# A third batch cut to 64 of 96 token rows, one-hot masks moved between two stages, and low weight halves made by accumulating DMAs

## The chip, the cores and the metric

The kernel runs on one core of a Trainium2 chip. The metric is device time in microseconds (us). A core has five engines that run side by side and meet at semaphores: TensorE (PE in the profile, PEld for its weight loads), VectorE (DVE), ScalarE (ACT), GpSimd (POOL) and SyncE (SP, which here only issues DMAs). Each engine works through its own instructions in their order; DMAs are issued from the queues of SP, ACT and POOL.

## The reference

```python
Y = np.fft.rfft(x, axis=1) * (filt_r + 1j * filt_i)[None]      # x: 8 batches x 3072 tokens x 256
x = np.fft.irfft(Y, n=3072, axis=1).reshape(8 * 3072, 256)     # the tokens of the second half
logits = x @ w_gate                                            # 8 experts
expert_idx = np.argmax(logits, axis=1)
gate_w = softmax(logits)[expert_idx]                           # per token
for i in range(N):                                             # in token order
    e = expert_idx[i]
    if counts[e] < capacity:                                   # 768 per expert
        disp[e, counts[e]] = x[i]; counts[e] += 1; keep[i] = True
y = relu(disp[e] @ w1[e]) @ w2[e]                              # 256 -> 1024 -> 256
out[i] = gate_w[i] * y[expert_idx[i], pos[i]] if keep[i] else 0
```

A convolution over each batch by Fourier transform, then a mixture of experts in which every expert takes its first 768 tokens and all other rows of the output are zero. So the kernel needs only as many tokens, from the start, as fill all eight experts. It transforms three of the eight batches, counts, and has a slow branch (`tc.If(least < cap)`) that does the other batches if some expert is not full by then.

## The kernel before, in words

**The transform.** A batch is 3072 tokens, laid out as 96 rows (`N1`) of 32 (`N2`). Token n is row n // 32, column n % 32. Six steps on TensorE, methods of `Conv`: `a` (matrix over the 96 rows), `t` (transposes), `b` (matrix over the 32 columns, then the complex product with the filter on DVE and POOL, lines 267 to 272), `g` (transpose back together with the gate matrix, so that 16 logit columns come along), `bi` (inverse over 32) and, outside the class, `ai` (inverse over 96, line 353), whose result is tokens in 96 rows. `ai` works in two halves of the 272 columns, `HS`: half 0 has 144 columns (128 channels and the 16 logit sums), half 1 has 128. ACT copies each bank of PSUM to an `rt` buffer (line 355, five buffers), SP stores it to `ybuf` in HBM (line 359), and for half 0 an addition makes the logits `L` (line 358). An fp32 matrix is recorded as two passes. Transposes of `V` (`ti`, line 342) on DVE stand between `bi` and `ai`. `middle` strings `b`, `g` and `bi` together and runs short lists of other work in ten places between, handed over as `fill`.

**Routing.** `route` returns steps: `counts` (maximum, one-hot and running sum of a batch on DVE), `sums` (two small matrices on TensorE that carry counts over rows and batches, line 410), `slots` (each token's place), four `masks` (one-hot matrices in fp16 for 8 of the 32 columns each, lines 455 to 457) and `table` (8 matrices for each mask, line 465, which scatter token numbers into the table `tacc` of slots).

**Experts.** A chunk is 384 slots of one expert; an expert has two, (e,0) and (e,1). `gather` fetches rows of `ybuf` by POOL's indirect DMAs, 128 at a time; `turn` transposes them and splits them into a high part in fp32r and a low part (the rest); `up_steps` multiplies with w1 in eight steps of six matrices, `down_steps` with w2 in three steps of 24, and a POOL DMA scatters the gated rows to the output. Each product is three matrices: high by high, low by high, high by low. The weights too are split: `load_part` loads a 1 MB matrix to `raw` and `cut` makes `wah`/`wbh` by a rounding copy on ACT (line 621) and `wal`/`wbl` by a subtraction (line 622) on POOL, or DVE if told so. For experts 0 and 1 a matrix is cut in four pieces, for later ones in two.

**Order.** The order is written out by hand (`manual_schedule`). The first chunks of experts 0 and 1 are filled after two batches, so they start early: in the third batch's stretch (lines 768 to 834) chunk (0,0) goes through its up and down matrices beside the last `ai`. Then (1,0), (0,1), (1,1) (lines 837 to 866), and from there `steady` takes experts 2 to 7, with the next expert's weights loaded and cut inside the up matrices of the current one.

## Time and profile before

| | |
|---|---|
| runs | 519.42 us median of 3 (518.61 to 519.8) |
| profiled execution | 519.1 us, its span 517.3 us |
| busy, share of the span | PE 95%, PEld 94%, DVE 48%, ACT 49%, POOL 47% |
| chain that ended last | PE 72%, issue 9%, POOL 6%, DVE 5%, ACT 4%, DMA 3% |
| POOL's DMA queue (q0) | 4608 packets, 12.98 MB |
| all DMAs | 81.32 MB, mean 157 GB/s |

Times in a trace count from the start of the span. A group of instructions is named by line, engine, operation, and the tiles it writes and reads (`ps<-V,AI`). A wait is put down to the instruction that ended it. The batches' transforms take the first 196 us, the early chunks run until 302.9 us, experts 2 to 7 from there to the end.

### The profile page before, as it was taken

Reading aid. Unit: us, or ns where it says so; the run is one execution under the profiler, and the core shown is the slowest. Engines: PE = TensorE matmul, PEld = TensorE weight load, DVE = VectorE, ACT = ScalarE, POOL = GpSimd, SP = SyncE. Lnnn points to the kernel's source line nnn. Section 1 sums busy time; section 2 is a strip of 40 time slices with the busy share of each in tenths; the row PEclk is TensorE's granted clock in tenths of the full one; section 3 lists DMA queues with packets and bytes.
Section 4 is the critical chain, followed back from the end, with each engine's and each line's share of the span. In section 5 each row is a group of like instructions: output and inputs, shape, how many; then the busy total and the mean of one; then the engine's idle time right before and its main releaser. Section 6 shows DMA issues by size and latency. Waiting matters only on the chain.

```text
span 517.3 us, 10377 instructions
## 1 busy us (share of the span) xinstructions
PE 493.3 (95%) x4076; PEld 484.7 (94%) x4076; DVE 245.7 (48%) x532; ACT 251.5 (49%) x603; POOL 243.2 (47%) x247
## 2 busy tenths in 40 slices
PE   8999999999999988799699999999999999999995
PEld 7989999999999888799698999999999999999995
DVE  0197744887557876952434234333342342333510
ACT  2535768356674657652335256235354362353421
POOL 2165110461104765538454478558367475673012
PEclk9999999999999999979899999999999999999999
DMA  8999770996818970574130344160160340611001
GB/s 226 318 339 406 257 210 17 246 406 241 236 41 284 406 255 12 159 204 130 49 125 22 108 153 143 42 238 22 42 238 32 91 167 32 204 56 54 10 23 46
DMA packets 52923, 81.32 MB, mean 157 GB/s; under 512 B 3969, under 2 KB 31873, under 8 KB 52737
## 3 DMA queue, kind: packets, MB, share of 16 engines
q1 hardware_dynamic: 39344, 53.95, 32.2%
q10 hardware_dynamic: 8912, 13.63, 8.2%
q0 software_dynamic: 4608, 12.98, 7.3%
q8 instruction: 34, 0.56, 0.5%
q14 instruction: 25, 0.20, 0.1%
HBM read 39.07 MB, written 41.48 MB: 156 GB/s over the span
## 4 chain that ended last, share of the span: by engine, by line
PE 72%; issue 9%; POOL 6%; DVE 5%; ACT 4%; DMA 3%; POOLq 0%; SPq 0%; ACTq 0%; DVEq 0%
PE ps L532 20%; PE ps L584 20%; PE ps L227 9%; PE ps L353 6%; PE ps L284 5%; PE ps L298 4%; PE ps L251 4%; POOL y L588 2%; DMA ybuf<-rt 2%; PE ps L499 1%; POOL wbl L622 1%; DVE t L267 1%; ACT Q L243 1%; DVE V L342 1%; DMA xt<-x 1%
## 5 line engine op out<-in xcount | busy, mean ns | idle before, releaser
L584 PE MATMUL ps<-wbh,h 128*128 128x256 f32 x768 | 139.7, 282 | 0.6 <-POOL h L513 0.6
L584 PEld LDWEIGHTS ps<-wbh,h 128*128 128x128 f32 x768 | 118.9, 189 | 1.4 <-POOL h L513 1.0
L515 DVE SCALAR_TENSOR_TENSOR h<-ps,h 128x384 fp32r<-128x384 f32 x120 | 65.6, 557 | 96.8 <-ACT h L507 89.1
L584 PE MATMUL ps<-wbl,h 128*128 128x256 f32 x384 | 107.7, 280 | 0.0
L532 PE MATMUL ps<-xh,wah 128*128 128x384 f32 x256 | 87.7, 342 | 4.5 <-ACT xh L507 4.5
L507 ACT ACTIVATE h<-ps 128x384 fp32r<-128x384 f32 x128 | 61.9, 497 | 56.7 <-PE ps L532 48.1
L532 PE MATMUL ps<-xl,wah 128*128 128x384 f32 x256 | 87.7, 343 | 0.7 <-DVE xl L517 0.5
L588 POOL DMA_INDIRECT y<-ob,idxs x48 | 47.7, 994 | 84.7 <-ACT ob L587 78.8
L532 PE MATMUL ps<-xh,wal 128*128 128x384 f32 x256 | 87.3, 341 | 0.0
L584 PEld LDWEIGHTS ps<-wbl,h 128*128 128x128 f32 x384 | 72.5, 189 | 0.0
L587 ACT ACTIVATE ob<-ps,gt 128x256 f32<-128x256 f32 x48 | 22.7, 473 | 82.1 <-PE ps L584 69.1
L271 POOL TENSOR_TENSOR t<-t,t 128x256 f32<-128x256 f32 x33 | 25.1, 759 | 63.2 <-DVE t L267 59.2
L532 PEld LDWEIGHTS ps<-xh,wah 128*128 128x128 f32 x256 | 49.1, 192 | 4.9 <-ACT xh L507 4.8
L353 PE MATMUL ps<-V,AI 128*96 128x144 f32 (+1 forms) x384 | 49.4, 287 | 1.6 <-DVE V L342 1.5
L532 PEld LDWEIGHTS ps<-xl,wah 128*128 128x128 f32 x256 | 48.9, 191 | 1.6 <-DVE xl L517 1.6
L353 PEld LDWEIGHTS ps<-V,AI 128*96 128x96 f32 x384 | 47.6, 168 | 2.3 <-ACT full L512 1.8
L532 PEld LDWEIGHTS ps<-xh,wal 128*128 128x128 f32 x256 | 49.0, 191 | 0.0
L485 POOL DMA_INDIRECT rows<-ybuf,idxg x42 | 42.4, 1011 | 12.5 <-issue 11.7
L622 POOL TENSOR_TENSOR wbl<-raw,wbh 128x1024 fp32r<-128x1024 f32 (+1 forms) x18 | 38.9, 2185 | 14.0 <-ACT wbh L621 13.9
L622 POOL TENSOR_TENSOR wal<-raw,wah 128x1024 fp32r<-128x1024 f32 (+1 forms) x19 | 37.6, 1998 | 16.6 <-issue 9.3
L287 ACT CAST yh<-ps 128x408 fp32r<-128x408 f32 x48 | 24.0, 500 | 42.8 <-PE ps L284 42.5
L517 DVE TENSOR_TENSOR xl<-ps,xh 128x384 fp32r<-128x384 f32 x30 | 15.1, 546 | 59.6 <-ACT xh L507 42.6
(119 smaller groups left out, 786.8 us busy)
## 6 DMA issues: line engine op xcount, KB each, us to landing
y<-zt SPq DMA_DIRECT2D x12, 2048.0 KB, 20.4
raw<-w ACTq DMA_DIRECT2D x13, 1024.0 KB, 9.6
xt<-x SPq DMA_DIRECT2D x20, 384.0 KB, 5.1
ybuf<-rt SPq DMA_DIRECT2D x30, 162.0 KB, 2.9
ybuf<-rt SPq DMA_DIRECT2D x24, 192.0 KB, 3.7
raw<-w SPq DMA_DIRECT2D x3, 1024.0 KB, 5.7
V<-x SPq DMA_DIRECT2D x4, 384.0 KB, 8.3
AI<-cai SPq DMA_DIRECT2D x1, 1536.0 KB
```

The source lines that it names most:

```text
L227: nc.tensor.matmul(ps[:, i * w:(i + 1) * w], xt[:, i, h * 128:(h + 1) * 128], A[:, i * QP:i * QP + w], start=True, stop=True)
L271: eng.tensor_tensor(out=t1[:, :, 0, :], in0=t1[:, :, 0, :], in1=t2[:, :, 1, :], op=ALU.subtract)
L284: nc.tensor.matmul(ps[:, i * 136:(i + 1) * 136], self.ysb[(p // 4, h)][:, (p % 4) * 128:(p % 4 + 1) * 128], self.IG[:, h, :], start=True, ...
L287: nc.scalar.copy(fh[:, o], ps[:, :408])
L353: nc.tensor.matmul(ps[:N1, i * w:(i + 1) * w], AI[:, n0 + i, :], V[h][:, :, n0 + i, :], start=True, stop=True)
L485: nc.gpsimd.indirect_dma_start(out=rows[:, t, :], out_offset=None, in_=yrows[:lim, :], in_offset=bass.IndirectOffsetOnAxis(ap=idx[:, j + t ...
L507: nc.scalar.activation(out=hi, in_=ps, func=f)
L515: nc.vector.scalar_tensor_tensor(out=lo, in0=ps, scalar=0.0, in1=hi.bitcast(F32), op0=ALU.max, op1=ALU.subtract)
L532: nc.tensor.matmul(ps[:, :n * 128], w[:, kk, m * 128:(m + 1) * 128], y[:, kk, o], start=k == 0, stop=k == 5)
L584: nc.tensor.matmul(ps[:, :D], y[:, m, o], w[:, m, :], start=m == 0 and j == 0, stop=m == NF - 1 and j == 2)
L588: ins = nc.gpsimd.indirect_dma_start(out=out, out_offset=bass.IndirectOffsetOnAxis(ap=(idxs if ix is None else ix)[:, j:j + 1], axis=0), i ...
L622: (eng or nc.gpsimd).tensor_tensor(out=fl, in0=r, in1=fh.bitcast(F32), op=ALU.subtract)
```

## The change

- Batch 2 (the third) ends in rows 0 to 63 alone, tokens 0 to 2047. New `ai_last` does columns j and j + 16 as a pair of matrices of 64 columns each, the first into partitions 0 to 63 of the bank and the second into 64 to 127. So the tile has 128 partitions and 16 columns, and the routing of that batch has half as many columns: two masks and 16 table matrices instead of four and 32. Its triangle and its token numbers come from a new input `co`.
- `cut` makes the low part another way: ACT writes the negated rounded copy, and after each half of a matrix a DMA from POOL's queue adds the fp32 weights from HBM onto it. There is no subtraction left on POOL or DVE.
- In every batch but the last, masks 0 to 3 and table pieces 0 and 1 stand between the steps of `ai`'s half 1, ahead of `middle`.
- In the middle of batch 2, the three gathers of chunk (0,0) stand in three places, and w2 of expert 0 is loaded and cut there; the early gate goes behind the up matrices.
- Behind it: all eight up steps of (0,0) first, then `ai_last`, with one down step of (0,0) between half 0 and half 1 and two more around the turn of (1,0). The loads of expert 1's matrices are issued earlier, on SP; its w2 is cut in four pieces, after steps 4 and 8 of the up matrices of (1,0) and of (0,1).
- The slow branch starts over from batch 0.

```diff
+    def ai_last(V, dst, h, L=None, eng=None):
+        c0, w = HS[h]
+        k, n2 = 512 // w, N2 // 2
+        def step(j0):
+            n = min(k, n2 - j0)
+            ps = bank()
+            for i in range(n):
+                for half in range(2):
+                    nc.tensor.matmul(ps[half * LAST:(half + 1) * LAST, i * w:(i + 1) * w], AI[:, half * n2 + j0 + i, :LAST],
+                                     V[h][:, :, half * n2 + j0 + i, :], start=True, stop=True)
+            rt = p1b.tile([128, 512], F32, name="rt", tag="rt", bufs=5)
+            nc.scalar.copy(rt[:, :n * w], ps[:, :n * w])
...
+            for half in range(2):
+                o = half * n2 + j0
+                nc.sync.dma_start(out=dst[:LAST, o:o + n, c0:c0 + w], in_=rv[half * LAST:(half + 1) * LAST])
...
             nc.scalar.copy(fh, r)
-            (eng or nc.gpsimd).tensor_tensor(out=fl, in0=r, in1=fh.bitcast(F32), op=ALU.subtract)
+            nc.scalar.activation(out=fl, in_=r, func=AF.Copy, scale=-1.0)
+            if (k + 1) * 2 % parts == 0:
+                n = shape[1] // 2
+                o = slice((k * 2 // parts) * n, (k * 2 // parts + 1) * n)
+                nc.gpsimd.dma_start(out=l[:, o, :], in_=src[:, o, :], accum_op=ALU.add)
...
-            interleave(halves[1][:6], masks[:2])
-            ahead = halves[1][6:]
-            fill = [[table[0], masks[2]], [table[1], masks[3]], [table[2]], table[3:]]
+            S = halves[1]
+            run([masks[0], masks[1], S[0], S[1], table[0], masks[2], S[2], S[3], table[1], masks[3], S[4], S[5]])
+            ahead = S[6:]
+            fill = [[table[2]], table[3:]]
...
-        fill[2].append(cut_a[0])
-        fill[3].append(early_rows)
-        fill += [[cut_a[1]], [lambda: cut_a[2](nc.vector)], [cut_a[3], load_b]]
+        fill[0].append(cut_a[0])
+        fill[1] += [early_index, cut_a[1]]
+        fill += [[cut_a[2], lambda: early_row(0, 0)], [cut_a[3], load_b, lambda: early_row(0, 1)], [lambda: early_row(0, 2)], [],
+                 [cut_b[0]], [cut_b[1]], [cut_b[2]], [cut_b[3]]]
...
-        run(early[:5])
+        run(early)
...
+        run(first)
+        run(cut_a[:1])
...
+        later[0]()
+        run(counts)
+        run(rest[:2])
+        sums()
+        run(cut_a[1:2])
+        run(rest[2:])
+        run(slots)
+        run(cut_a[2:])
+        load_b, cut_b = load_part(1, "b", raw0, w1p, 4, nc.sync)
+        load_b()
+        later[1]()
+        run(masks)
+        X[1, 0] = turn(early_x[1], NE, ep1)
+        later[2]()
         run(table)
...
-        up((1, 0), [cut_b[0]], 1)
+        up((1, 0), [lambda: None, cut_b[0], lambda: None, cut_b[1]], 1)
         prep((0, 1))
-        up((0, 1), [cut_b[1]], 0)
+        up((0, 1), [lambda: None, cut_b[2], lambda: None, cut_b[3]], 0)
```

Three places of the order, in rows of the programs (number, line, operation, output<-inputs, size, count). First TensorE behind the third batch's middle; `V_116` and `V_117` are the halves of the columns, L532 and L570 are the up matrices, L622 the down matrices, `pr` the counts, L499 the turn. Before:

```order
703 L532 MATMUL ps<-xh,wal 128x384
704 L353 MATMUL ps<-V_116,AI 96x144 x32
705 L353 MATMUL ps<-V_117,AI 96x128 x20
706 L410 MATMUL pr<-sc,tri 96x8
707 L411 MATMUL pr<-tot,ones 96x8
708 L353 MATMUL ps<-V_117,AI 96x128 x12
709 L499 MATMUL ps<-ident,rows_2680 128x64 x12
```

Now:

```order
723 L570 MATMUL ps<-xh,wal 128x384
724 L383 MATMUL ps<-V_116,AI 64x144 x32
725 L622 MATMUL ps<-wbh,h 128x256
...
741 L622 MATMUL ps<-wbh,h 128x256
742 L383 MATMUL ps<-V_117,AI 64x128 x16
743 L448 MATMUL pr<-sc,both 128x8
744 L449 MATMUL pr<-tot,ones 128x8
745 L383 MATMUL ps<-V_117,AI 64x128 x16
746 L622 MATMUL ps<-wbh,h 128x256
```

As many matrices as before, of 64 rows of output instead of 96, and a down step of chunk (0,0) on either side of half 1.

Second, POOL from the end of that middle to expert 1's w2; `wal` and `wbl` are the low parts, L485 and L523 the gathers, L588 and L626 the scatters, `h` the low part of the up result. Before:

```order
93 L513 TENSOR_TENSOR h<-full,h 128x384 x5
94 L485 DMA rows_2680<-ybuf,idx_72 128x272 x3
95 L622 TENSOR_TENSOR wbl<-raw,wbh 128x512 x4
96 L513 TENSOR_TENSOR xl<-full,xh 128x6x64 x2
97 L513 TENSOR_TENSOR h<-full,h 128x384 x3
98 L622 TENSOR_TENSOR wal<-raw,wah 128x512 x4
99 L588 DMA y<-ob,idxs_73 24576x256 x2
100 L485 DMA rows<-ybuf,idxg 128x272 x6
101 L588 DMA y<-ob,idxs_73 24576x256
102 L622 TENSOR_TENSOR wbl<-raw,wbh 128x1024 x2
```

Now:

```order
95 L664 DMA wbl<-w 128x4x256
96 L551 TENSOR_TENSOR h<-full,h 128x384 x8
97 L523 DMA rows_2723<-ybuf,idx_72 128x272 x3
98 L389 TENSOR_TENSOR L<-rt 128x24 x5
99 L389 TENSOR_TENSOR L<-rt 128x8
100 L626 DMA y<-ob,idxs_73 24576x256
101 L664 DMA wal<-w 128x1024 x2
102 L626 DMA y<-ob,idxs_73 24576x256 x2
103 L523 DMA rows<-ybuf,idxg 128x272 x6
104 L664 DMA wbl<-w 128x4x256 x2
```

Subtractions have become DMAs in POOL's queue, between gathers and scatters, and the logit additions of the third batch have come from DVE.

Third, ACT in the up matrices of (0,1), behind the turn: `h` is the eviction of a step, L621 and L659 the rounding copies, L660 the negated ones, `ob` the eviction of down of (1,0). Before:

```order
265 L551 ACTIVATE lg<-lg 128x24
266 L507 ACTIVATE h<-ps 128x384 x2
267 L621 CAST wbh<-raw 128x1024
268 L507 ACTIVATE h<-ps 128x384 x6
269 L616 DMA raw<-w 128x2x1024
270 L587 ACTIVATE ob<-ps,gt 128x256 x3
```

Now:

```order
285 L589 ACTIVATE lg<-lg 128x24
286 L545 ACTIVATE h<-ps 128x384 x4
287 L659 CAST wbh<-raw 128x512
288 L660 ACTIVATE wbl<-raw 128x512
289 L545 ACTIVATE h<-ps 128x384 x4
290 L659 CAST wbh<-raw 128x512
291 L660 ACTIVATE wbl<-raw 128x512
292 L654 DMA raw<-w 128x2x1024
293 L625 ACTIVATE ob<-ps,gt 128x256 x3
```

The last cut of expert 1's w2 stood behind the second step of these eight and now stands behind the eighth, right ahead of the down matrices that use it.

## Rows read from the trace of the kernel before

**Rows 1.** Stages: length, busy us (count) by engine, TensorE clock, DMA share, GB/s.

```profile
core 0 of [0], span 517.3 us
...
91.10:125.60 34.50, 34.50 (x314) 34.29 (x313) 28.31 (x52) 17.89 (x65) 16.83 (x23) 1.00 0.96 328
157.90:196.60 38.70, 35.85 (x326) 34.92 (x324) 31.59 (x60) 20.33 (x67) 24.17 (x29) 1.00 0.81 289
196.60:241.10 44.50, 39.06 (x301) 37.16 (x300) 28.51 (x68) 24.20 (x57) 25.31 (x23) 0.92 0.42 115
241.10:302.90 61.80, 56.70 (x411) 55.12 (x409) 21.10 (x57) 25.23 (x51) 31.57 (x25) 0.94 0.30 96
302.90:337.70 34.80, 34.80 (x265) 34.60 (x265) 12.63 (x32) 15.92 (x32) 25.55 (x19) 1.00 0.34 112
```

**Rows 2.** TensorE's waits, 157 to 303 us: total us, times, longest us.

```profile
PE ps L532 <- ACT xh L507: 4.5, 2, 3.6
PE pr L410 <- DVE sc L406: 3.1, 1, 3.1
PE ps L284 <- POOL t L272: 2.8, 2, 2.0
PE ps L353 <- DVE V L342: 1.5, 1, 1.5
```

**Rows 3.** Chain of waits, TensorE's pieces: start us, us, engine, line, count.

```profile
66.10 7.89 PE ps L353 x64
...
152.47 5.45 PE ps L353 x48
...
236.59 1.40 PE pr L465 x32
...
249.48 1.79 PE ps L499 x12
...
254.75 10.97 PE ps L532 x47
...
274.20 0.56 PE ps L499 x12
...
276.34 8.52 PE ps L532 x47
...
302.88 16.65 PE ps L532 x96
319.53 8.54 PE ps L584 x72
328.07 0.89 PE ps L499 x24
```

**Rows 4.** Timeline, DVE: start us, us, operation, count, idle before and releaser.

```profile
198.68 5.04 DVE L342 STREAM_TRANSPOSE V<-V 128x2304 f32<-128x2304 f32 x2 [0.28 <-ACT V L300]
...
220.61 0.16 DVE L415 COPY bs<-pr 96x8 f32<-96x8 f32 x1 [0.90 <-PE pr L411]
...
238.03 0.20 DVE L470 TENSOR_TENSOR tacc<-tacc,pr 128x48 f32<-128x48 f32 x1 [9.52 <-PE pr L465]
```

**Rows 5.** Timeline, ACT, same columns: expert 0's w2 cuts; stores of batch 2.

```profile
212.95 2.18 ACT L621 CAST wbh<-raw 128x512 fp32r<-128x512 f32 x4
...
225.64 1.96 ACT L355 COPY rt<-ps 96x512 f32<-96x512 f32 x3 [8.10 <-DMA ybuf<-rt]
```

**Rows 6.** Lines of POOL: count, then busy us, mean ns, idle before.

```profile
L622 POOL TENSOR_TENSOR wal<-raw,wah 128x1024 fp32r<-128x1024 f32 (+1 forms) x19 | 37.6, 1998 | 16.6 <-issue 9.3 <-ACT wah L621 7.4
...
L485 POOL DMA_INDIRECT rows<-ybuf,idx x6 | 6.2, 1035 | 1.5 <-issue 0.9 <-DVE t L267 0.3 <-DVE te L603 0.2
```

**Rows 7.** DMA issues: count, KB each, median us from issue to landing.

```profile
raw<-w ACTq DMA_DIRECT2D x13, 1024.0 KB, 9.6
...
raw<-w SPq DMA_DIRECT2D x3, 1024.0 KB, 5.7
...
ybuf<-rt SPq DMA_DIRECT2D x3, 108.0 KB, 2.3
```

More of the change, by code (lines that the diff above doesn't have):

```diff
@@ L75, in dft_constants, with order_constants, fftconv_moe_kernel @@
     return f32(A), f32(AI), f32(B), freq
+def order_constants():
+    half, row = np.divmod(np.arange(128), LAST)
+    before = row * 2 + half
+    tri = (before[:, None] < before[None, :]).astype(np.float32)
+    token = 32 * row[:, None] + N2 // 2 * half[:, None] + np.arange(N2 // 2)[None, :] - N1 * N2 // 2
+    return np.ascontiguousarray(np.concatenate([tri, token], 1), dtype=np.float32)
 @with_exitstack
-def fftconv_moe_kernel(ctx, tc, x, fr, fi, fny, wg, w1, w2, ca, cai, cb, out, cap):
+def fftconv_moe_kernel(ctx, tc, x, fr, fi, fny, wg, w1, w2, ca, cai, cb, co, out, cap):
     nc = tc.nc
@@ L371, in pad_V, with new_L @@
             nc.gpsimd.memset(v[:, :, NP:N2, :], 0.0)
-    def new_L():
-        return p1b.tile([N1, N2, E], F32, name="L", tag="L", bufs=1)
+    def new_L(last=False):
+        return (es if last else p1b).tile([128, N2 // 2, E] if last else [N1, N2, E], F32, name="L", tag="L", bufs=1)
+    rc = {}
     def route(L, last, ohp):
-        t = lambda nm, sh, dt=F32: p1b.tile(sh, dt, name=nm, tag=nm, bufs=1)
+        P, T = (128, N2 // 2) if last else (N1, N2)
+        t = lambda nm, sh, dt=F32: (es if last else p1b).tile(sh, dt, name=nm, tag=nm, bufs=1)
+        mask, tri, nv = rc["last" if last else "all"]
+        w8, iol, ioh, ones = (a[:P] for a in rc["same"])
         st = {}
@@ L616, in load, with cut @@
             (dma or nc.scalar).dma_start(out=box[0], in_=src)
[L618 removed]
+        def cut(k):
             w = shape[1] * shape[2] // parts
@@ L621, in cut @@
             nc.scalar.copy(fh, r)
-            (eng or nc.gpsimd).tensor_tensor(out=fl, in0=r, in1=fh.bitcast(F32), op=ALU.subtract)
-        return load, [lambda eng=None, k=k: cut(k, eng) for k in range(parts)]
+            nc.scalar.activation(out=fl, in_=r, func=AF.Copy, scale=-1.0)
[3 more added lines that the diff above has]
+                nc.gpsimd.dma_start(out=l[:, o, :], in_=src[:, o, :], accum_op=ALU.add)
+        return load, [lambda k=k: cut(k) for k in range(parts)]
     def load_w(e, raw, pool):
@@ L676, in early_count @@
     def early_count():
-        nc.vector.tensor_tensor(out=tot[:, E:], in0=tot[:, :EE], in1=lack.to_broadcast([N1, EE]), op=ALU.add)
+        nc.vector.tensor_tensor(out=tot[:, E:], in0=tot[:, :EE], in1=lack.to_broadcast([128, EE]), op=ALU.add)
     def full_flag():
         ps = bank()
-        nc.tensor.matmul(ps[:1, :E + EE], ones[:, 0:1], tot, start=True, stop=True)
+        nc.tensor.matmul(ps[:1, :E + EE], rc["same"][3][:, 0:1], tot, start=True, stop=True)
         nc.vector.tensor_reduce(out=cmin, in_=ps[:1, :E + EE], axis=AX.X, op=ALU.min)
```

151 lines of the change are left out of this document (74 added, 77 removed).

## The prediction

> **What bounds the kernel now.** I read the table of stages first [rows 1], since a time bound by TensorE can only fall where TensorE idles, runs at a lower clock, or has less to do. The middle of batch 1 takes 34.5 us with TensorE busy throughout. The same work for batch 2 takes 38.7 us and leaves 2.85 us idle. From there to expert 1's first matrix is 44.5 us with 5.4 us idle at a mean clock of 0.92, then 61.8 us with 5.1 us idle at 0.94. A steady expert (34.8 us) has no gap. So the room is in the 145 us from 157.9 to 302.9 and nowhere behind it. The waits of TensorE there [rows 2] name the ends that came last: the activation of turned rows, the scan of the routing counts, and POOL's complex additions in the middle. The chain of waits [rows 3] gives the price of each piece of matrix work and the two places where the turned rows come late. The DVE, ACT and POOL rows [rows 4 to 6] show what stood in front of those ends: one ACT copy waited 8.10 us for the DMA that empties its `rt` buffer, because SP's queue was held by a weight load.
>
> The sum is made against the profiled execution, 519.1 us with a span of 517.3 [rows 1] (1.8 us around it); the median shown is 519.42, 0.3 above, and I do not correct for that. Runs of this kernel tell a change from none at about 0.2%, 1 us.
>
> **The middle of batch 2.** Two of the four one-hot masks and two of the four table pieces leave it for the copy-back before it. TensorE's order only changes, so the same work fits 34.5 us plus one turn, 0.45 (24 transposes take 0.89 [rows 3]): 35.0 against 38.7 [rows 1]. What goes is DVE's load (31.59 us busy against 28.31 in batch 1), three POOL subtractions and one on DVE; what comes is on POOL, between its additions: four accumulating DMAs, two of them of 512 pieces of 1 KB, and the three gathers, now one at a time. The trace has no plain DMA issued by POOL; the nearest row is a gather of 128 rows, 1035 ns [rows 6], so I bound an issue by nothing (added work can't gain) and by 4 us (four times the pieces), and take 1.0 for the halves of w1 and 1.5 for those of w2. Then POOL carries 3 x 1.3 for gathers and 5.0 for DMAs, against 3 x 1.3 and 3 x 1.3 before (512 columns, a little over half of the mean 1998 [rows 6]). Each DMA also waits for ACT's two copies, and the next additions stand behind it in POOL's queue; TensorE waits for those. ACT doubles its cuts: eight of 1.1 us (2 x 0.55, four took 2.18 [rows 5]) against four of 0.55; they fall between evictions. I leave 1.1 us of the stall: 36.1, **-2.6** (bounds 0 and -3.7).
>
> **From the middle to expert 1's first matrix, 44.5 us.** The path is TensorE's own order now. Expert 0's eight up steps: 48 x 0.173 = 8.3 (96 in 16.65 [rows 3]). The inverse transform: before, half 0 is 64 passes at 123 ns, 7.9 (64 in 7.89), half 1 is 64 at 114, 7.3 (48 in 5.45). The number of passes stays, each with 64 columns, two by two on the left and right half of the array. If a pair runs at the same time this costs half, 7.6; if not, 15.2. No row shows a pair of fp32 matrix passes; the nearest are the turns, whose 64-wide transposes alternate between the halves: 0.89/24 = 37 ns each [rows 3], where a column at the inverse's price (123/144 = 0.85 ns) would give 55 for 64. That is a factor of 1.5 as it stands, though a transpose may be cheaper for itself. I take 1.7: 8.9.
> The Trainium skill's TensorEngine Tiling (Array Packing), under Key Properties, says that tiles load weights and multiply independently, which by itself gives a factor of 2 here, and that a change of tiling mode drains the engine, which speaks against the new order, since it changes shape six times. By the factor of 2 the sum would be 1.3 us lower; the turns' rows neither show a drain nor exclude one.
> The rest: expert 0's down matrix, 8.5 (72 in 8.54), of which one step now stands after half 0 and one between half 1 and the turn; one turn 0.45; counts and flag 0.5; the table 0.7 (half of 1.40 for 32). Sum 8.3 + 8.9 + 8.5 + 0.45 + 0.5 + 0.7 = 27.4.
> Waits in it: DVE's four transposes of V start 2.1 us after the first up matrix (198.68 against 196.6) and take 5.04 for the first two [rows 4], so some 9.8 in all. Before, V was late (1.5 us [rows 2]); now eight up steps stand ahead instead of five and half 0 finds its V. New is that ACT's exponential of the early gate waits for DVE behind those transposes, until about 12.6 us, and the six `rt` copies of half 0 stand behind it; TensorE has seven banks and six steps, so it goes on, but POOL's additions to L, and so the counts on DVE, end near 18, and TensorE comes for them at 8.3 + 4.7 + 2.8 + 2.1 = 17.9. A miss here is 0 to 2 us. The scan that cost 3.1 us [rows 2] is half as long and no longer under POOL's subtractions. Slots and four masks took 7.9 us (220.61 to 238.03 less the 9.52 that DVE then waited [rows 4]); with two masks they end at some 24, TensorE needs them at 26. The 8.10 us wait of ACT [rows 5] goes, since the weight load is issued ahead of the stores. What is late next is the low half of expert 1's w1: its second accumulating DMA is issued after ACT's fourth cut at about 22 and lands near 27, where TensorE wants it. I add 1.5 us for these: 28.9, **-15.6** (bounds -18, pairs at a factor of 2 and no wait, and -9, no pairs).
>
> **From there to the steady loop, 61.8 us.** The matrix work is unchanged: three ups of 8.3, two downs of 8.5 and one of 8.7, and four turns of 0.45: 52.4. Before lost 9.4: the turn at 249.48 took until 254.75 (5.27), the up behind it 10.97 instead of 8.3 at the lower clock, the turn at 274.20 until 276.34 (2.14) [rows 3]. After: two turns of 2.14, so 1.7 lost twice. And one new wait. The last quarter of expert 1's w2 is cut by ACT only after the eighth up step of (0,1), and the second accumulating DMA follows it; before, the last cut stood behind the second step. Down of (1,0) starts at once and wants that half at its 14th matrix, 1.5 us in. The DMA: eviction 0.5, two copies 1.1, POOL issue 1.0, landing. Landings in the trace: 108 KB in 2.3 us, 1 MB in 5.7 or 9.6 [rows 7]; 512 KB by the first two 3.8, which I take, and by the first and last 5.5; bounds 2.3 and 9.6. So it lands at 6.4, a stall of 4.9 (bounds 3.4 and 10.7). Everything of TensorE is queued behind it. A wait of 3.6 us [rows 2] was followed by the slow up (2.6 us lost, clock 0.94 over the stage); I charge 2.3. Together 52.4 + 3.4 + 4.9 + 2.3 = 63.0, **+1.2** (bounds -6, no new wait and full clock, and +7, the late landing).
> The Trainium skill's DMA: Bandwidth & Descriptors (the anatomy of a GpSimd DMA) fits such a transfer as 2.0 us plus bytes over 436 GB/s: an estimate of 3.2 us for 512 KB, and a sum 0.6 us lower. No row here has an accumulating transfer.
>
> **The steady experts.** POOL's subtractions (37.6 us for the 19 of w1 [rows 6], about as much for w2) become DMAs; POOL is not on TensorE's path there. ACT gets 4 x 1.05 us more per expert (a quarter is twice the 0.55 us piece) inside an up of 8.3, 4 us of evictions and 8 of cuts, 12 in all, and falls some 3 us behind; seven banks and the following down cover that. Low parts are needed 17 us after their cut. Cost 0.
> Leaving 32 of 96 rows means 8192 tokens are routed instead of 9216; worked out from the reference's inputs, the smallest expert gets 845 of them, over the 768 wanted, so the slow branch stays unused.
>
> **Sum:** 519.1 - 2.6 - 15.6 + 1.2 = **502.1 us**.
>
> **Rivals.** (1) Pairs do not overlap: 15.2 instead of 8.9, 6.3 more, 508.4. For it: no fp32 pair in the trace. Against: 37 ns per transpose. (2) Low weights come early: half landing as the small stores do and no clock lost, 5 us less, and the middle free of stalls, 1 less: 496. Before's own turn stall at 249 had no cause that I can name, so waits here can also vanish. (3) POOL is the new bound: 4 us per w2 issue in the middle and the late weights at their upper ends: 502.1 + 3.7 + 6 = 512. (4) Slower: the accumulating DMAs are bound by their rate. Each steady expert sends 2 MB on one queue in which the gathers and scatters stand behind; the loop has 34.8 us for it. If 2 MB take longer, every one of the five rounds takes that time: the gain is eaten at 38.2 us, and 40 give 5 x 5.2 = 26 more, 528. The weight loads' 9.6 us per MB make it 19; the accumulation would have to double that.
>
> **How the numbers follow.** Forecast 0.48, rival 1 0.16, rival 2 0.20, rival 3 0.09, rival 4 0.07. Range 493 to 512: rival 2's side down to 493, rival 3's up to 512; the forecast's own terms give 498 to 507. Faster 0.90, same 0.03 (rival 3 at its worst), slower 0.07.
>
> **What would show it.** The 128 passes of the third batch in under 9 us (pairs) or about 15; no `rt` copy on ACT that waits 8 us for a DMA; expert 1's first matrix near 223 us; a wait of TensorE for DMA `wbl` of some 5 us in down of (1,0), about 20 us later; steady rounds still 34.8 us. Steady rounds over 35.5 us, or a middle above 39, would prove it wrong.

## The result, and the profile after

The changed kernel takes 515.16 us (median; 511.63 to 517.97) against 519.59 for the kernel before in the same comparison: a ratio of 0.9915, 95% interval 0.9895 to 0.9935. The forecast was 502.1 with a range of 493 to 512, so the measured time lies outside it. The direction was right; of 17 us, 4.4 came. The profiled execution below took 511.6 us (span 509.9), the fastest of the 20, 3.5 under the median. The medians and ratios given further down leave out the seven executions, of four of the kernels, that took over 1.5% longer than the fastest of the same kernel.

Stages of the changed kernel, cut at the same events as [rows 1] (same columns):

```profile
core 0 of [0], span 509.9 us
...
91.40:124.90 33.50, 33.50 (x299) 33.47 (x298) 24.62 (x46) 17.87 (x65) 16.30 (x23) 1.00 0.99 337
157.90:194.50 36.60, 35.15 (x309) 34.09 (x309) 25.81 (x54) 26.24 (x82) 24.22 (x30) 1.00 0.98 294
194.50:223.00 28.50, 27.76 (x285) 26.11 (x283) 19.71 (x42) 18.83 (x45) 16.53 (x22) 1.00 0.88 222
223.00:295.20 72.20, 58.56 (x411) 56.45 (x410) 23.23 (x71) 30.01 (x61) 26.23 (x25) 0.91 0.51 127
295.20:330.00 34.80, 34.80 (x266) 34.59 (x265) 12.60 (x32) 20.13 (x37) 19.53 (x19) 1.00 0.88 201
```

Against [rows 1]: the middle of batch 2 36.6 instead of 38.7, the stage up to expert 1's first matrix 28.5 instead of 44.5, and then 72.2 instead of 61.8. The steady expert is the same, 34.8. So 18.1 us were gained by 223 us, more or less where and as the sum had them, and 10.4 lost again in the 72 us behind. TensorE's waits of that time, columns as in [rows 2]:

```profile
PE ps L622 <- DMA wbl<-w: 6.5, 1, 6.5
PE ps L570 <- DMA wal<-w: 3.7, 1, 3.7
PE ps L570 <- ACT xh L545: 2.9, 2, 2.0
PE ps L294 <- POOL t L282: 1.4, 4, 0.7
PE pr L448 <- DVE sc L444: 0.6, 1, 0.6
```

None of the ends of [rows 2] is left at its old size, and the two that are new at the top are accumulating DMAs for the second halves of expert 1's `wal` (L570 is up) and `wbl` (L622 is down). Their issues on POOL, and the matrices that waited (start us, us, count, idle before and releaser):

```profile
219.85 0.89 POOL L664 DMA_DIRECT2D wal<-w  x1 [2.10 <-ACT wal L660]
...
250.82 1.32 POOL L664 DMA_DIRECT2D wbl<-w  x1 [10.12 <-ACT wbl L660]
```

```profile
228.02 0.44 PE L570 MATMUL ps<-xh,wal 128*128 128x384 f32 x1 [3.74 <-DMA wal<-w]
...
256.96 0.55 PE L622 MATMUL ps<-wbl,h 128*128 128x256 f32 x1 [6.49 <-DMA wbl<-w]
```

From the start of POOL's issue to the matrix that needed it: 8.2 and 6.1 us. POOL had waited for ACT's copies each time, so the DMAs were issued late, and they land slowly. Behind each of these two waits TensorE's clock is at half. Here are its windows around the second (us, PE busy, granted clock, DMA):

```profile
250.00:252.00 2.00, 0.48 (x5) 1.00 0.75 236
252.00:256.00 4.00, 0.00 (x0) 0.59 1.14 263
256.00:260.00 4.00, 3.04 (x14) 0.50 0.39 117
260.00:264.00 4.00, 4.00 (x25) 0.63 0.09 33
264.00:266.00 2.00, 2.00 (x20) 1.00 0.00 0
```

After the wait, 3.0 us of work run at 0.50 (1.2 GHz) and 4 at a mean of 0.63: 1.5 + 1.5 = 3.0 us lost beside the 6.5 of the wait. Behind the wait for `wal` it is 1.7 (4 us at 0.60 and 5 at 0.98). The turn of (0,1) waits 2.0 us at 239.9, and the clock stays at 1.00 behind it.

The end of the third batch, in passes:

```profile
203.37 4.18 PE L383 MATMUL ps<-V,AI 128*64 128x144 f32 x64
...
210.49 1.98 PE L383 MATMUL ps<-V,AI 128*64 128x128 f32 x32
...
213.62 1.99 PE L383 MATMUL ps<-V,AI 128*64 128x128 f32 x32
```

8.15 us, where the 64 + 64 passes cost 7.9 and 7.3 before by [rows 3]; the forecast had 8.9.

In the middle there is a wait that the prediction did not have. ACT's first cut of expert 0's w2 waits for the load (the load's row is from the chain of waits):

```profile
171.43 9.33 DMA raw<-w
```

```profile
180.78 0.62 ACT L659 CAST wbh<-raw 128x512 fp32r<-128x512 f32 x1 [2.94 <-DMA raw<-w]
181.30 0.63 ACT L660 ACTIVATE wbl<-raw 128x512 fp32r<-128x512 f32 x1
181.84 0.88 ACT L297 CAST yh<-ps 128x408 fp32r<-128x408 f32 x2
```

The load is issued at 171.4, when the fourth cut of w1 has freed the only `raw` buffer, and lands 9.3 us later; the evictions `yh` that the middle needs are queued behind the cut. What holds the load up at first stands in the DMA queues between 171.43 and 174 (packets, MB, share of 16 engines; q0 is POOL's queue, q1 carries SP's):

```profile
q0 software_dynamic: 141, 0.52, 100.4%
q1 hardware_dynamic: 7, 0.01, 1.1%
```

The engines are full with what POOL issued before, above all the accumulating DMA for expert 0's w1 of 167.06, which itself stood behind a zero fill that SP had issued at 163.49. The load's data move from 174 on.

### The profile page after: what moved, and what is told of

Read it like the earlier page. It is cut to its first block, busy times and chain, and to the rows that moved or that the text cites. A ratio compares the mean times of both kernels' runs of the same rounds, so it can differ in the third digit from the quotient of the medians.

```text
span 509.9 us, 10387 instructions
## 1 busy us (share of the span) xinstructions
PE 483.3 (95%) x4060; PEld 474.4 (93%) x4060; DVE 234.2 (46%) x519; ACT 275.7 (54%) x634; POOL 203.3 (40%) x246
## 4 chain that ended last, share of the span: by engine, by line
PE 59%; issue 19%; POOL 9%; DMA 5%; ACT 3%; DVE 3%; POOLq 1%; another core or an unknown queue 0%; SPq 0%; DVEq 0%
PE ps L622 14%; PE ps L570 13%; PE ps L237 9%; PE ps L363 6%; PE ps L294 5%; PE ps L261 5%; PE ps L308 4%; POOL y L626 4%; POOL rows L523 3%; DMA raw<-w 2%; DMA ybuf<-rt 2%; PE ps L383 1%; DMA wbl<-w 1%; ACT Q L253 1%; PE ps L537 1%
## 5 line engine op out<-in xcount | busy, mean ns | idle before, releaser
L622 PE MATMUL ps<-wbh,h 128*128 128x256 f32 x768 | 142.0, 285 | 0.0
L622 PEld LDWEIGHTS ps<-wbh,h 128*128 128x128 f32 x768 | 121.2, 192 | 0.8 <-issue 0.2
L622 PE MATMUL ps<-wbl,h 128*128 128x256 f32 x384 | 109.0, 284 | 6.5 <-DMA wbl<-w 6.5
L570 PE MATMUL ps<-xh,wal 128*128 128x384 f32 x256 | 87.1, 340 | 3.7 <-DMA wal<-w 3.7
L570 PE MATMUL ps<-xh,wah 128*128 128x384 f32 x256 | 87.3, 341 | 2.9 <-ACT xh L545 2.9
L570 PE MATMUL ps<-xl,wah 128*128 128x384 f32 x256 | 87.2, 341 | 0.6 <-DVE xl L555 0.5
L626 POOL DMA_INDIRECT y<-ob,idxs x48 | 48.7, 1014 | 84.4 <-ACT ob L625 77.2
L622 PEld LDWEIGHTS ps<-wbl,h 128*128 128x128 f32 x384 | 73.9, 192 | 6.7 <-issue 6.7
L570 PEld LDWEIGHTS ps<-xh,wal 128*128 128x128 f32 x256 | 48.6, 190 | 4.3 <-DMA wal<-w 4.1
L570 PEld LDWEIGHTS ps<-xh,wah 128*128 128x128 f32 x256 | 48.5, 190 | 3.3 <-ACT xh L545 3.2
L523 POOL DMA_INDIRECT rows<-ybuf,idxg x42 | 43.2, 1028 | 18.8 <-issue 11.9
L570 PEld LDWEIGHTS ps<-xl,wah 128*128 128x128 f32 x256 | 48.7, 190 | 1.4 <-DVE xl L555 1.4
L281 POOL TENSOR_TENSOR t<-t,t 128x256 f32<-128x256 f32 x33 | 25.0, 757 | 61.2 <-DVE t L277 56.8
L555 DVE TENSOR_TENSOR xl<-ps,xh 128x384 fp32r<-128x384 f32 x32 | 16.2, 547 | 60.5 <-ACT xh L545 55.6
L294 PE MATMUL ps<-IG,t 128*128 128x136 f32 x288 | 38.7, 281 | 2.5 <-POOL t L282 2.5
L237 PEld LDWEIGHTS ps<-A,xt 96*128 96x128 f32 x320 | 38.7, 203 | 1.3 <-issue 1.3
L237 PE MATMUL ps<-A,xt 96*128 96x128 f32 x320 | 39.1, 286 | 0.6 <-DMA xt<-x 0.6
L294 PEld LDWEIGHTS ps<-IG,t 128*128 128x128 f32 x288 | 35.5, 190 | 3.7 <-POOL t L282 3.7
```

The lines of the kernel that those rows point to most:

```text
L237: nc.tensor.matmul(ps[:, i * w:(i + 1) * w], xt[:, i, h * 128:(h + 1) * 128], A[:, i * QP:i * QP + w], start=True, stop=True)
L281: eng.tensor_tensor(out=t1[:, :, 0, :], in0=t1[:, :, 0, :], in1=t2[:, :, 1, :], op=ALU.subtract)
L294: nc.tensor.matmul(ps[:, i * 136:(i + 1) * 136], self.ysb[(p // 4, h)][:, (p % 4) * 128:(p % 4 + 1) * 128], self.IG[:, h, :], start=True, ...
L523: nc.gpsimd.indirect_dma_start(out=rows[:, t, :], out_offset=None, in_=yrows[:lim, :], in_offset=bass.IndirectOffsetOnAxis(ap=idx[:, j + t ...
L570: nc.tensor.matmul(ps[:, :n * 128], w[:, kk, m * 128:(m + 1) * 128], y[:, kk, o], start=k == 0, stop=k == 5)
L622: nc.tensor.matmul(ps[:, :D], y[:, m, o], w[:, m, :], start=m == 0 and j == 0, stop=m == NF - 1 and j == 2)
```

## The experiments

Theory A: what is missing was lost to the late low weights of expert 1, as wait and as half clock. Theory B: the rows of (0,1), which need the last stores of batch 2, are the floor, so a wait taken away comes back at the turn. Theory C: accumulating DMAs are late because the DMA engines are full. All times of a group were taken on one chip with the kernel before beside them; its median was 514 to 519 us from chip to chip, so kernels of different groups are compared by their ratio. The changed kernel itself came out at 0.9915, 0.9956 and 0.9932 on three chips, so a difference of 0.4% between groups shows nothing. The groups are again to sub_all, both to zeros, mid_later to masks_back, and again2 to best3. Of every profile: the middle of batch 2 (TensorE's first `L261` to expert 0's first up matrix), from there to expert 1's first, from there to the first of (1,1), ACT's wait for the load of w2, and TensorE's longest waits for `wal` and `wbl`.

| kernel | median us | ratio (95%) | middle | to (1,0) | to (1,1) | ACT's wait | wal, wbl |
|---|---|---|---|---|---|---|---|
| before | | | 38.8 | 44.4 | 34.7 | | |
| changed | 515.2 | 0.9915 (0.9895-0.9935) | 36.7 | 28.4 | 45.4 | 2.9 | 3.7, 6.5 |
| again | 512.2 | 0.9956 (0.9924-0.9988) | 39.8 | 28.6 | 42.8 | 4.2 | 2.8, 6.4 |
| w1_sub | 508.8 | 0.9895 (0.9865-0.9924) | 35.8 | 31.5 | 39.3 | 1.8 | none, 6.5 |
| w2_early | 502.9 | 0.9782 (0.9744-0.9819) | 39.9 | 28.7 | 36.4 | 5.9 | 3.0, none |
| sub_all | 502.8 | 0.9780 (0.9750-0.9810) | 39.8 | 31.3 | 30.0 | 3.2 | none |
| both | 504.3 | 0.9705 (0.9676-0.9733) | 39.1 | 31.3 | 33.8 | 5.1 | none |
| filler | 511.3 | 0.9847 (0.9823-0.9871) | 35.8 | 28.8 | 44.0 | 1.5 | 4.2, 0.2 |
| load_later | 516.0 | 0.9923 (0.9899-0.9947) | 40.1 | 28.8 | 46.2 | 4.6 | 4.2, 6.5 |
| zeros | 513.6 | 0.9896 (0.9857-0.9934) | 38.7 | 28.4 | 46.1 | 4.7 | 3.8, 6.5 |
| mid_later | 513.3 | 0.9878 (0.9856-0.9899) | 36.1 | 28.7 | 47.4 | none | 4.3, 6.7 |
| best2 | 508.3 | 0.9781 (0.9762-0.9800) | 36.0 | 36.7 | 34.3 | none | none, 0.6 |
| unpaired | 514.8 | 0.9928 (0.9902-0.9955) | 37.4 | 29.3 | 46.9 | 3.4 | 2.3, 6.6 |
| masks_back | 513.2 | 0.9889 (0.9869-0.9908) | 36.6 | 28.5 | 46.2 | none | 3.7, 6.3 |
| again2 | 511.4 | 0.9932 (0.9899-0.9965) | 36.5 | 29.3 | 42.5 | 2.5 | 2.7, 6.9 |
| e1_sub | 499.8 | 0.9720 (0.9675-0.9765) | 35.9 | 29.8 | 30.0 | 1.9 | none |
| e1_move | 497.4 | 0.9680 (0.9647-0.9713) | 36.8 | 29.1 | 30.2 | 3.0 | none |
| best3 | 497.5 | 0.9671 (0.9644-0.9698) | 36.1 | 29.1 | 31.8 | none | none |

**again** (first group: the changed kernel itself, as a level).

> The changed kernel unchanged, as the level for the others of this call. Both theories: ratio to before 0.99 (0.9915 so far), profile with a wait of TensorE for wal of about 3.7 us after 224 and one for wbl of about 6.5 us after 250, each followed by some us at half clock. If the profiled run of this call is not among its fastest ones, these waits or the half-clock stretches should be longer by the difference (the first profile, 511.6 us, was 3.5 under the median).

The two waits are there again, 2.8 and 6.4 us. Its middle takes 39.8 us where the first profile had 36.7: ACT waits 4.2 us for w2 instead of 2.9.

**w1_sub**

```diff
             nc.scalar.copy(fh, r)
+            if e == 1 and part == "a":
+                nc.gpsimd.tensor_tensor(out=fl, in0=r, in1=fh.bitcast(F32), op=ALU.subtract)
+                return
             nc.scalar.activation(out=fl, in_=r, func=AF.Copy, scale=-1.0)
```

> Expert 1's w1 alone is cut as before the change (low part = raw minus rounded copy, on POOL), everything else as changed. Theory A (late low weights: each wait and the half clock behind it is lost time): the wait of 3.7 us for wal goes and 1.7 us at half clock with it, 5.4 us less than 'again'. Theory B (the rows of (0,1) are the floor: last stores of batch 2, then index, gathers, turn): the stores land some 2 us sooner at best, the gathers' rows are there at 234 to 236, TensorE has done up (1,0) at 231 and waits 3 to 5 us for the turn instead: 0 to 2 us less than 'again'.

3.3 us less than again, between the two. The wait for `wal` is gone and no longer wait at the turn took its place (2.8 us at turns in both), so B falls. The third stretch is 3.5 us shorter than again's, but 2.9 of it are paid in the second (e1_move shows what for); the middles of these two profiles, 35.8 against 39.8, differ too, though the edit does not touch them.

**w2_early**

```diff
-        up((1, 0), [lambda: None, cut_b[0], lambda: None, cut_b[1]], 1)
+        up((1, 0), [lambda: None, cut_b[0], cut_b[1], cut_b[2]], 1)
         prep((0, 1))
-        up((0, 1), [lambda: None, cut_b[2], lambda: None, cut_b[3]], 0)
+        up((0, 1), [cut_b[3]], 0)
```

> The four cuts of expert 1's w2 stand after steps 4, 6 and 8 of up (1,0) and step 2 of up (0,1), instead of 4, 8 and 4, 8. Theory A: the second accumulating DMA is issued near 243 instead of 250.8, lands before 250.5, so the wait of 6.5 us goes and 3 us at half clock behind it: 9.5 us less than 'again'. Theory C (accumulating DMAs land late because the DMA queues are full, not because they are issued late): its landing moves by less than its issue, a wait of 3 us or more stays: 3 to 5 us less. ACT gets behind in up (1,0) by two cuts (2.2 us); if its evictions then hold up the turn, 2 us of the gain are lost.

9.3 us less than again, as A had it. The second accumulating DMA starts at 247.0, 3.8 us sooner than the changed kernel's, though TensorE begins up (0,1) some 1.8 us later than there, and the wait is gone. The profile shows less of it, 6.4 us in the third stretch: here the clock is at half from 243.5 to 246.9, behind a wait of 1.9 us at the turn, which again's profile has too, at full clock.

**sub_all** (the same edit with `if True`)

> All weights are cut by the subtraction on POOL as before the change, the rest (pairs, masks, new order) as changed. Theory A: both waits go, 14 to 15 us less than 'again' behind the middle; in the middle POOL has eight subtractions of 1.3 us instead of four DMAs of about 1.2, 1 to 3 us more: 11 to 14 us less in all, near 502, and steady rounds 0.1 us shorter. Theory B: w1's part gives nothing, 8 to 10 us less. If neither wait matters by itself: within 1 us of 'again'.

9.4 us less than again, short of A's 11 to 14; by the time alone it is what B forecast. The profile speaks for A: both waits are gone and the third stretch is 30.0, the shortest of its group. What is missing stands ahead of it: the second stretch is 2.7 us longer than again's (as in w1_sub), and the middle, with POOL's eight subtractions in it, is at 39.8. The steady rounds stay at 34.8 to 35.1.

**both** (w1_sub and w2_early)

> w1_sub and w2_early together (expert 1's w1 cut by subtraction on POOL, w2's cuts earlier). If the two waits are separate losses they add up: w1_sub was 0.6% under 'again', w2_early 1.7%, so 2.3% under it, a ratio to before of about 0.972. If TensorE, coming 4 us earlier, then meets the second half of wbl before it has landed, a wait of 2 to 4 us comes back: ratio 0.977 to 0.980.

The first case: 0.9705. The third stretch, 33.8, still holds a wait of 3.8 us for ACT at the turn of (0,1), with three cuts instead of two in ACT's order ahead of it. That the third cut is the reason is not shown: w2_early has the same order and waits 1.9 there, but TensorE comes to it later, after its wait for `wal`.

**filler**

```diff
         R[2, 0] = load_rows(2, 0)
+        ps = bank()
+        for i in range(54):
+            nc.tensor.matmul(ps[:, :D], H[1, 0][0][:, 0, :128], W[1][2][:, 0, :], start=True, stop=True)
         down((1, 0), idxs0)
```

> The changed kernel with 54 matrices of 128x256 (117 ns each, 6.3 us) that nobody reads, ahead of down (1,0): TensorE works where it waited 6.5 us for wbl; the DMA is as late as before. If the half clock behind the wait is a cost of its own, it doesn't come, and the 3 us of it are gained: 0.6% under the changed kernel. If the half clock has another cause, or the 6.3 us of work are dearer than the wait, the time is that of the changed kernel or up to 2 us more.

0.9847 against the changed kernel's 0.9915, with intervals that don't meet (again's and again2's are higher still; that of zeros, of the same group, meets it by 0.0014), and 6.4 us of work added that nobody needs. TensorE's windows in it:

```profile
250.00:252.00 2.00, 2.00 (x19) 1.00 0.39 31
252.00:256.00 4.00, 4.00 (x36) 1.00 1.01 308
256.00:260.00 4.00, 3.84 (x32) 1.00 0.74 174
260.00:264.00 4.00, 4.00 (x36) 1.00 0.09 33
```

The DMA is as late as before (the wait left is 0.2 us), and the clock stays at 1.00 where it was 0.50 and 0.63. So the half clock is a cost of its own that the idle time brings, not the late DMA. How much of the 0.7% is due to it is less sure: the middle was a short one in this profile (35.8), and the third stretch, 44.0, lies within the 42.5 to 47.4 of the kernels with both waits. Behind `wal` this profile lost more than the changed kernel's: 4.9 us of work at half clock after a wait of 4.2.

**load_later**

```diff
-        load_a()
         R[2, 0] = load_rows(2, 0)
-        down((1, 0), idxs0)
+        later = down_steps((1, 0), idxs0)
+        later[0]()
+        load_a()
+        run(later[1:])
```

> The changed kernel with expert 2's w1 (1 MB, issued by ACT at 249.0, 1.8 us ahead of the late accumulating DMA) loaded behind the first step of down (1,0). If the 512 KB land 6 us after their issue because they share the DMA engines with that load, they land 2 to 3 us sooner and the wait of 6.5 us for wbl falls to 3.5 to 4.5: 0.4 to 0.6% under the changed kernel. If an accumulating DMA takes that long by itself, the wait stays within 0.5 us.

No change, 0.9923. POOL issues at 256.65, the matrix goes on at 262.82: 6.2 us, and 6.1 with the 1 MB load beside it. C falls for this DMA as far as other transfers are meant: 512 KB accumulated take some 6 us from the start of the issue without that load too. The windows of this run show what they are made of (last two columns: share of the DMA engines, GB/s):

```profile
256.00:258.00 2.00, 0.31 (x3) 0.10 (x1) 0.00 (x0) 0.35 (x1) 1.32 (x1) 1.00 0.00 0
258.00:259.00 1.00, 0.00 (x0) 0.00 (x0) 0.00 (x0) 0.00 (x0) 0.72 (x1) 1.00 0.26 34
259.00:260.00 1.00, 0.00 (x0) 0.00 (x0) 0.00 (x0) 0.00 (x0) 0.69 (x2) 0.66 0.83 112
260.00:261.00 1.00, 0.00 (x0) 0.00 (x0) 0.00 (x0) 0.00 (x0) 0.75 (x1) 0.50 1.21 195
```

Nothing moves in the first 1.4 us, and then this one transfer fills the DMA engines by itself at 195 GB/s; in the changed kernel a zero fill moves 403 GB/s at a share of 1.04 (166 to 169 us). So the engines are full, but with the accumulating DMA itself, at about half the rate.

**zeros**

```diff
             run(halves[0])
+            if b + 2 == NB0:
+                zero_out(2)
...
-        cv.middle(V, with_zeros(fill, (2, 3, 4, 5)), ahead, last=[early_turn])
+        cv.middle(V, with_zeros(fill, (2, 5), 2), ahead, last=[early_turn])
```

> The changed kernel with two of the four 2 MB zero fills of batch 2's middle issued in the copy-back stage of batch 1 (near 140, where the DMA engines are idle), so that one instead of three stands right behind the load of expert 0's w2 in SP's queue. In the two profiles of the changed kernel ACT's first cut of that w2 waits 2.9 and 4.2 us for the load (which lands after 9.3 and 10.7 us), and the middle takes 36.7 and 40.1 us. If the fills delay the load: it lands in some 6 us, ACT's wait goes, the middle takes 35.5 to 36.5 in every profile, 1 to 3 us less than the changed kernel, with less spread from run to run. If the load is slow for another reason: no change.

No change: ACT waits 4.7 us for the load and the middle is 38.7. Two fewer zero fills behind the load do not speed it. The run leaves the fill ahead of the load (issued at 163.96) and the accumulating DMA behind that where they were. (The 40.1 us above for the second profile is 39.8 by the table's cut.)

**mid_later**

```diff
-                 [cut_b[0]], [cut_b[1]], [cut_b[2]], [cut_b[3]]]
+                 [], [cut_b[0]], [cut_b[1]], [cut_b[2], cut_b[3]]]
```

> The changed kernel with the four cuts of expert 0's w2 one place later in batch 2's middle (places 7, 8, 9, 9 instead of 6 to 9). In nine profiles so far ACT's first cut of it waits 1.5 to 5.9 us for its load, which takes 8 to 12 us to land, and the middle takes 35.8 us where the wait is short and 39 to 40 where it is long. If that wait is what the middle loses: it falls under 3 us, the middle takes 35.8 to 37, 2 to 3 us less in the median than the changed kernel and runs that lie closer together. If POOL's four accumulating DMAs between the additions are what it loses: no change, 39 to 40.

Half right. ACT's wait is gone and the middle takes 36.1; over all profiles with these cuts and the masks where the change put them and a fast load (ACT's wait up to 2.5 us) it takes 35.8 to 36.5, with 4 us and more 38.7 to 40.1. But the ratio, 0.9878, is only 0.4% under the changed kernel's 0.9915: in this profile 2 us came back in the third stretch (47.4). There the turn of (0,1) waits 3.0 us instead of 2.0, and 3.4 us at half clock follow it (242.7 to 246.1), which the changed kernel's first profile does not have; load_later, zeros, unpaired and masks_back have them too.

**best2** (w2_early, mid_later, and the cuts of expert 1's w1 earlier)

```diff
+        run(cut_a[:2])
         early_gate(0)
         last_fill()
         run(first)
-        run(cut_a[:1])
+        run(cut_a[2:])
...
-        run(cut_a[1:2])
...
-        run(cut_a[2:])
```

> All low weights still by accumulating DMAs, but each cut early enough: w2 of expert 0 as in mid_later, w1 of expert 1 with two cuts ahead of the copies of half 0 and two behind them (instead of one behind half 0 and three spread to the end of half 1), w2 of expert 1 as in w2_early. If lateness of the cuts is the whole loss: no wait for wal or wbl, w2_early's 1.7% and some 5 us more for wal with its half clock, and 2 us in the middle: 3.3 to 3.6% under before. If accumulating DMAs and loads get into each other's way wherever they stand: a wait of 2 us or more for one of them stays, 2.5%.

2.2% instead of 3.3 to 3.6. The waits for low weights are gone, but w1 had not landed when ACT came to its first cut. ACT, DVE and TensorE one after the other:

```profile
206.59 0.62 ACT L659 CAST wah<-raw 128x512 fp32r<-128x512 f32 x1 [3.12 <-DMA raw<-w]
...
215.60 0.28 ACT L386 COPY rt<-ps 128x144 f32<-128x144 f32 x1 [4.62 <-DMA ybuf<-rt]
```

```profile
216.19 0.29 DVE L422 TENSOR_REDUCE mx<-L 128x16 f32<-128x128 f32 x1 [6.31 <-POOL L L389]
```

```profile
218.28 0.60 PE L448 MATMUL pr<-sc,both 128*128 128x8 f32 x2 [6.69 <-DVE sc L444]
```

ACT waited 3.1 us for the load ahead of the copies of half 0, took 2.2 us for the two cuts, and then waited 4.6 us, at the last of these copies, for the store of an `rt` buffer; this put the counts off until TensorE waited 6.7 us for them. An earlier cut is no gain when its load is not there. Why the store was late is open.

**unpaired**

```diff
-            for i in range(n):
-                for half in range(2):
+            for half in range(2):
+                for i in range(n):
                     nc.tensor.matmul(ps[half * LAST:(half + 1) * LAST, i * w:(i + 1) * w], AI[:, half * n2 + j0 + i, :LAST],
```

> The changed kernel with the same 64-column matrices of the third batch's end, but in each bank all of the left half of the array first, then all of the right. In the changed kernel 64 passes take 4.18 us and twice 32 take 1.98, 8.1 in all. If pairs overlap because neighbours stand on different halves: about 123 ns each again, 15.5 in all, 7 to 7.5 us more than the changed kernel, less what waits behind it absorb (the 3.7 us for wal hang on ACT's copies, so at most 1 to 2). If 64-column matrices are short by themselves: no change.

```profile
203.71 4.48 PE L383 MATMUL ps<-V,AI 128*64 128x144 f32 x64
...
211.16 2.59 PE L383 MATMUL ps<-V,AI 128*64 128x128 f32 x32
...
214.25 2.59 PE L383 MATMUL ps<-V,AI 128*64 128x128 f32 x32
```

9.66 us instead of 8.15, not 15.5: the order in pairs gives 1.5 us, and 64 output columns instead of 96 give the rest of the 7.1 us against before, 5.5, in either order. (A bank still changes halves once in the middle, so some overlap there is not excluded.) The 1.5 us did not show in the time (0.9928); TensorE's wait for `wal` is 2.3 us instead of 3.7.

**masks_back**

```diff
-            run([masks[0], masks[1], S[0], S[1], table[0], masks[2], S[2], S[3], table[1], masks[3], S[4], S[5]])
-            ahead = S[6:]
-            fill = [[table[2]], table[3:]]
+            interleave(halves[1][:6], masks[:2])
+            ahead = halves[1][6:]
+            fill = [[table[0], masks[2]], [table[1], masks[3]], [table[2]], table[3:]]
...
```

> The changed kernel with the one-hot masks and table pieces of batches 0 and 1 where they were before (two masks and all four table pieces inside the middle), the early index and gathers two to three places later for it. If DVE's load in the middle is what the move saves: batch 1's middle takes 34.5 instead of 33.5 and batch 2's 2 us more than the changed kernel's, 2.5 to 3 us in all. If the late load of w2 hides it: only batch 1's 1 us.

Batch 1's middle takes 34.6 instead of 33.5 as before the change, batch 2's 36.6; in time it is no slower (0.9889). What leaves the middle stands in the copy-back, so moving the masks by itself gains nothing that can be measured. On batch 2's middle it decides nothing, since the load of w2 came early in this run and ACT did not wait.

**again2, e1_sub, e1_move, best3** (one group). e1_sub is w1_sub's edit with `if e == 1`. e1_move and best3 have e1_sub's edit and this one (best3 mid_later's too):

```diff
-        run(cut_a[:1])
...
         run(rest[:2])
         sums()
-        run(cut_a[1:2])
+        run(cut_a[:2])
```

> The changed kernel unchanged, on the chip of this call, as the level for the next three: 0.991 to 0.996 of before. In the profile TensorE waits 3 to 4 us for wal and 6.5 for wbl; the middle of batch 2 takes 36 to 40 us, with ACT's wait for the load of w2 between 1.5 and 6 us.

> Both matrices of expert 1 cut by subtraction on POOL at the changed kernel's places; all other weights by accumulating DMAs. If the late DMAs for expert 1 alone are the loss: the stretch from expert 1's first matrix to (1,1) takes 30 us as in sub_all (there all weights were subtracted), against 43 to 47, and POOL's first subtraction stretches a DVE operation ahead of the counts, 3 us more ahead of it (31.4 instead of 28.5): 11 to 13 us under the changed kernel. If sub_all's 30 us came from having no accumulating DMA anywhere: 34 or more, as with both.

> e1_sub with the first cut of expert 1's w1 behind the first two copies of half 1 instead of ahead of the counts. In w1_sub, both and sub_all a DVE operation of the counts takes 1.40 us instead of 0.29, from the same moment as POOL's subtraction of 1.29 us, TensorE then waits 2.0 us for the counts and runs the next matrices at half clock. If DVE is held up by POOL: the operation takes 0.29 again, the stretch 28.5 to 29.5 instead of 31.4, 2 to 3 us under e1_sub. If it was ACT that came late: no change.

> e1_move and the later cuts of expert 0's w2 (mid_later). Middle 36, then 29, 30 and 26.8 us: steady experts from 280, 8 us earlier than with both; ratio to before 0.953 to 0.962. If a wait removed in the middle comes back behind it, as in mid_later (47.4 us there against 45.4): the same as e1_move within 1 us.

e1_sub: 499.8 against again2's 511.4, 11.6 us, the first case: the DMAs for expert 1 alone make up the loss. Its stages from expert 0's first matrix on, at a clock of 1.00 throughout:

```profile
194.90:224.70 29.80, 27.63 (x284) 25.99 (x282) 23.79 (x42) 17.00 (x41) 19.63 (x23) 1.00 0.91 247
224.70:254.80 30.10, 27.34 (x195) 26.21 (x193) 14.20 (x40) 13.20 (x29) 17.98 (x17) 1.00 0.36 111
254.80:281.50 26.70, 26.47 (x217) 26.01 (x218) 9.51 (x32) 14.60 (x28) 10.26 (x11) 1.00 0.48 120
```

30.1 + 26.7 = 56.8 us where the changed kernel takes 72.2 and the kernel before 61.8.

In e1_sub DVE is held up ahead of the counts, in e1_move it isn't (POOL's subtraction and DVE's comparison of e1_sub, then the comparison of e1_move):

```profile
211.91 1.29 POOL L661 TENSOR_TENSOR wal<-raw,wah 128x512 fp32r<-128x512 f32 x1 [0.31 <-ACT wah L659]
```

```profile
211.95 1.39 DVE L426 TENSOR_TENSOR sc<-L,mx 128x128 f32<-128x128 f32 x1
```

```profile
211.96 0.29 DVE L426 TENSOR_TENSOR sc<-L,mx 128x128 f32<-128x128 f32 x1
```

TensorE's wait for the counts falls from 2.0 to 0.9 us and the stretch from 29.8 to 29.1. The ratios, 0.9720 and 0.9680, have intervals that overlap; the mechanism is shown, its worth in time is not. In w1_sub the matrices behind the wait of 2.0 us ran at half clock for 3.4 us, in e1_sub at full clock, so the second stretch is 31.5 there and 29.8 here. best3 is the same as e1_move within 1 us, the second case of its expectation, so mid_later's gain is not to be seen in the median here either: its third stretch is 1.6 us longer than e1_move's, with 3.4 us at half clock behind a wait of 1.3 us at the turn. These two beat both kernels: 3.2 to 3.3% under the one before, and 2.7% under the changed one of this group (497.4 against 511.4).

## Why the prediction was wrong

**Up to expert 1's first matrix it held.** Middle: -2.1 in the profile against -2.6. The next stage: 28.5 against 28.9. The ups, the counts, ACT's wait for `ybuf` (2.1 us instead of 8.10) and the passes (8.15 against 8.9) came out. The reason given for the passes did not: they were cheap mostly because they are narrow (5.5 us of 7.1), and the order in pairs gave 1.5. That 8.9 came close is luck; rival 1 with its 15.2 us for passes that don't pair was wrong on the same point. The Trainium skill's TensorEngine Tiling (Array Packing), Key Properties, has tiles multiply independently and a change of mode drain the engine. Independence alone would make the order matter by a factor of 2; the order gives 9.66 against 8.15, so the trace does not bear that out as the reason. Of the six changes of shape five show no wait, and the 0.6 us at the other are put down to DVE's counts.

**The step that failed is "From there to the steady loop", +1.2, which measured +10.4.** Its 63.0 us were 52.4 of work, 3.4 for the turns, 4.9 for `wbl` and 2.3 for the clock. Measured: the turns as forecast (2.1 and 1.1 us). The wait for `wbl` 6.5, since issue and landing took 6.1 instead of 4.8 (the issue 1.3 where the sum took 1.0, though it had put 1.5 for the same kind in the middle; the landing 4.8 where it took 3.8). The half clock 4.7 (3.0 and 1.7). And a wait of 3.7 us for `wal`, which had been put at 1.5, ahead of this stage: ACT's fourth cut was to stand near 22 us into the stage before and ended 25.0 into it, because the cuts are queued behind the copies of half 1, the first of which waits 2.1 us for a store, and the DMA then took 8 us, not 5. The sum 52.4 + 3.2 + 6.5 + 4.7 + 3.7 = 70.5 leaves 1.7 of the 72.2: the three ups take 8.9 to 9.1 us each beside wait and clock, instead of 8.3, and the downs 0.4 less in all. The mechanism was named, as forecast and as rival 3; the error was to charge the clock once for two waits, to allow 1.5 us for the wait for `wal` and all others of the stage ahead, and to take the landing from plain stores and loads. The Trainium skill's DMA: Bandwidth & Descriptors (the anatomy of a GpSimd DMA) fits a DMA as 2.0 us plus bytes over 436 GB/s, an estimate of 3.2 us for 512 KB; the 6.1 and 8.2 us from issue to use of these accumulating transfers are far from it, and the measurements decide. e1_sub shows the size of the step: with these DMAs away the stage takes 56.8 us, 15.4 under the changed kernel and 6.2 under the forecast's 63.0, which had 7.2 of wait and clock in it. That its ratio, 0.972 (0.967 for best3), comes near the forecast's 502.1/519.1 = 0.967 is therefore luck and no proof of the sum; the kernel before was faster on that chip too (514.8).

**A term was missing in the middle.** The prediction counted ACT's copies there and not their load. ACT's first cut of w2 waits 1.5 to 5.9 us for it, and the middle ranges from 35.8 to 40.1 us, beyond the bound of 38.7 that was given. This, and the 1.7 us of half clock behind the turn that mid_later's profile has and the changed kernel's has not, can make the difference of 3.5 us between the profiled run and the median; that they do was not shown run by run. Why the load takes 8 to 12 us in most runs is shown in part: its data start 2.5 to 2.8 us after the issue where expert 0's w1 is cut by accumulating DMAs (1.9 in masks_back, with the gathers later), and 1.2 after it in sub_all, which has no such DMAs and where it landed after 6.7 us. No run takes away expert 0's DMAs alone, or the zero fill ahead of them.

**Rivals.** 2 (waits vanish) and 4 (steady rounds longer than 38 us) fell: the rounds take 34.8 to 35.1. Rival 3 was nearest, for the late weights at the upper end, though 515.2 lies beyond its 512 too; its other half, POOL's issue at 4 us, fell: 0.9 to 1.5.

## What to carry to other kernels

Moving work off a compute engine onto a DMA makes its result later: ask for each piece when its first reader comes, and count the last producer in its queue, the issue and a measured landing of the same kind of transfer, not of the nearest plain one. A wait of TensorE can be paid twice, when the matrices behind it run at half clock: here the waits of 2.8 to 6.9 us all were, and of those of 1.3 to 2.7 us some were and some not. Where such a wait can't be avoided, work put in front of it can cost nothing: the 6.4 us of matrices that nobody reads made this kernel no slower. Where a change gains early in a program, look behind it for the first thing that was just in time before.
